# A fused attention and channel-mix kernel: its first wide product by Strassen's identity, with the tokens in rows of 512

## The chip, the cores and the metric

The kernel runs on one core of a Trainium2 chip. The metric is the device time of one launch in microseconds (us), taken as the median of several runs. The profiled execution is one launch more, whose trace gives the rows below.

The engines are called as in the profile: PE is TensorE (matmuls), PEld its weight loads, DVE is VectorE, ACT is ScalarE, POOL is GpSimd, and SP is the engine that issues the transfers (DMAs).

## The reference, cut to what matters

All data are float32, in 4 batches of 576 tokens, 512 channels wide.

```python
x = attention(q, k, v)                 # 8 heads, window 32, half of them dilated
xk = mu_k * x + (1 - mu_k) * x_prev    # xr alike, with mu_r
k = np.maximum(xk @ w_k, 0.0)          # 512 x 1024
x = sigmoid(xr @ w_r) * (k * k @ w_v)  # 512 x 512, 1024 x 512
h = x.transpose(0, 2, 1) @ U @ V       # 576 x 32, 32 x 576
u = x + h.transpose(0, 2, 1)
out = u + np.maximum(u @ w_ch1, 0.0) @ w_ch2   # 512 x 2048, 2048 x 512
```

The last line is phase two. Its two products are the widest of the kernel, and the first of them, `u @ w_ch1`, is the one that the change computes in another way.

## The kernel before

Channels lie on the partitions and tokens in the rows, so that a matmul takes 128 x 128 weights and as many columns as it has tokens. To keep float32 precision every operand is split into a high part (an ACT copy that rounds) and a low part (the difference, on DVE or POOL), and every product is three matmuls: high weights by high tokens, low by high, high by low (`mm3`, lines 309 to 311).

The tokens come in 8 half batches of 288 (`HS`, counted by `c`). Phase one does the attention and the products with w_r, w_k and w_v; its result y goes to DRAM (`ytmp`). U and V come between: for a batch, `load_y` reads y back (`yb`), `y_tr` transposes it (line 822), `u_mm` multiplies by U (lines 840, 841), and `v_mm` (line 855) multiplies by V and adds y, which gives u. Here u, its high part `uh` and its low part `ul` stay in SBUF.

Phase two is a loop over the 8 half batches and, within one, over the 16 blocks `f` of 128 hidden channels. `ch1(c, f)` is 12 matmuls 288 wide (4 pieces of 128 input channels, three matmuls each) into a PSUM bank of the kind `psM`. ACT takes the high part of its relu (line 894, `ch`), DVE the low part (line 895, `cl`). `ch2(c, f)` is 12 more matmuls, 3 for each of 4 output blocks (lines 914 to 916, four `psS` banks). It stands one block behind, so that ACT and DVE have the time of 24 matmuls. After the 16th block DVE adds u (line 922) and SP writes `ot` out (line 924). The split weights of both products are made once (`load_w2`, lines 298, 300, 303) and stay in SBUF for all half batches.

The order on each engine is not written by hand. Each operation goes on a list with a cost, and a planner (`plan`) deals the list out to five queues (PE, ACT, DVE, POOL, SP); each engine then works in that order and waits where an operand or a buffer isn't there yet. All transfers are issued by SP, one queue, in order. Buffers are taken in turn from pools: a tile with `bufs` of 2 waits for the readers of the one two before it.

Of the kernel before, what the change touches and what calls it, by code (L numbers as in the profile page):

```python
# [16 lines left out]
P = 128  # L17
# [41 lines left out]
W2RATE = 0.35  # L59
SPLIT = (-4, -4, -3, -3, -1, -1, 0, 0, 1, 1, 2, 2, 5, 5, 6, 6, 7, 7, 8, 8)  # L60
# [13 lines left out]
def tile_attention_mix_channel(  # L74
# [49 lines left out]
    def plan():  # L124
# [283 lines left out]
    def w2_part(i, part):
        t, c, _ = parts2[i][part]
        return t()[:, c : c + CW]  # L410

    def w2_keys(i, *parts):
        return [parts2[i][part][2] for part in parts]

    def load_w2(i, eng):
        st = Lazy([P, 2 * CW], F32, "w64", "wst", 4)
        dma(P * CW * 8, lambda: nc.sync.dma_start(st(), w2f[i]), [("w2f", i, 0), ("w2f", i, 1)], [(st,)])
        parts2[i] = [place2(4 * i + part) for part in range(4)]
        for j in range(2):
            hi_lo(CW, lambda j=j: st()[:, j * CW : (j + 1) * CW], [(st,)],  # L420
                  lambda j=j: w2_part(i, j), w2_keys(i, j), lambda j=j: w2_part(i, 2 + j), w2_keys(i, 2 + j), eng)
# [743 lines left out]
```

## Time and profile before

| | |
|---|---|
| median of the runs before | 793.4 us (790.64, 793.4, 795.26) |
| span of the profiled execution | 791.1 us |
| phase two begins | about 380 us |
| PE busy | 759.7 us, 96% of the span |
| DVE, ACT, POOL busy | 387.1, 326.0, 207.2 us |
| moved by DMA | 77.68 MB |

The span is the profiled execution's own time from its first to its last instruction. The runs are timed without a profile, and their median lies 2.3 us above this span. A busy PE means only that a matmul was under way: matmuls are pipelined, a new one starts long before the one ahead has ended, so the rate is read from the starts.

### The profile page before, as it was taken

How to read it: one execution, taken by the hardware profiler on the slowest of the kernel's cores; microseconds unless marked ns; L12 is line 12 of the kernel's file. 1: busy time of each engine (PE TensorE's matmuls, PEld its weight loads, DVE VectorE, ACT ScalarE, POOL GpSimd, SP SyncE). 2: the span in 40 equal slices, each digit the busy share in tenths (PEclk: the TensorE clock that was granted, in tenths of full speed). 3: DMA queues.
4: the chain of work that ended last, by engine and by line, in shares of the span. 5: the costliest groups of instructions: out<-in, count | busy, mean ns of one | idle time of the engine just before them, and what ended most of it. 6: DMA issues, size and time to landing. Idle time of an engine off the chain costs nothing.

```text
span 791.1 us, 16047 instructions
## 1 busy us (share of the span) xinstructions
PE 759.7 (96%) x6360; PEld 734.5 (93%) x6360; DVE 387.1 (49%) x1013; ACT 326.0 (41%) x875; POOL 207.2 (26%) x234
## 2 busy tenths in 40 slices
PE   5788999989999999999999999999999999999997
PEld 4566899989899999999999999999999999999997
DVE  5899999998989754464412322122221222221211
ACT  5577786767677676364311212112211112121110
POOL 1333365655465556292100011000101001010000
PEclk8999999999999999999999999999999999999999
DMA  8687348786777270128002000020000000000000
GB/s 256 201 244 221 106 134 236 236 254 193 243 218 224 92 248 1 44 94 276 28 1 90 1 31 2 1 90 1 1 31 1 30 2 1 31 2 1 31 1 31
DMA packets 34764, 77.68 MB, mean 98 GB/s; under 512 B 3968, under 2 KB 12288, under 8 KB 34688
## 3 DMA queue, kind: packets, MB, share of 16 engines
q1 hardware_dynamic: 34688, 76.65, 30.8%
q8 instruction: 50, 0.82, 0.4%
q14 instruction: 26, 0.21, 0.1%
HBM read 58.81 MB, written 17.83 MB: 97 GB/s over the span
## 4 chain that ended last, share of the span: by engine, by line
PE 80%; DVE 8%; ACT 6%; DMA 3%; issue 2%; POOL 1%; SPq 0%; DVEq 0%; ACTq 0%; POOLq 0%
PE psS L916 9%; PE psS L915 9%; PE psM L309 9%; PE psM L311 9%; PE psM L310 9%; PE psS L914 9%; PE psM L729 7%; PE psM L731 7%; PE psM L730 7%; ACT pr L594 2%; DMA w<-w1raw 2%; DVE wl L300 2%; PE psS L637 1%; PE psM L726 1%; PE psS L575 1%
## 5 line engine op out<-in xcount | busy, mean ns | idle before, releaser
L894 ACT ACTIVATE ch<-psM 128x288 fp32r<-128x288 f32 x128 | 52.6, 411 | 324.8 <-PE psM L311 322.8
L895 DVE SCALAR_TENSOR_TENSOR cl<-psM,ch 128x288 fp32r<-128x288 f32 x128 | 58.4, 456 | 248.5 <-ACT ch L894 248.5
L914 PE MATMUL psS<-ch,w 128*128 128x288 f32 x384 | 114.4, 298 | 0.0
L916 PE MATMUL psS<-cl,w 128*128 128x288 f32 x384 | 113.7, 296 | 0.0
L309 PE MATMUL psM<-uh,w 128*128 128x288 f32 x384 | 113.2, 295 | 0.0
L311 PE MATMUL psM<-ul,w 128*128 128x288 f32 x384 | 113.1, 295 | 0.0
L915 PE MATMUL psS<-ch,w 128*128 128x288 f32 x352 | 103.8, 295 | 0.0
L310 PE MATMUL psM<-uh,w 128*128 128x288 f32 x352 | 103.5, 294 | 0.0
L729 PE MATMUL psM<-xk,wh 128*128 128x288 f32 x336 | 101.2, 301 | 0.0
L731 PE MATMUL psM<-xk,wh 128*128 128x288 f32 x336 | 99.0, 295 | 0.9 <-POOL xk L298 0.9
L730 PE MATMUL psM<-xk,wl 128*128 128x288 f32 x336 | 99.2, 295 | 0.0
L914 PEld LDWEIGHTS psS<-ch,w 128*128 128x128 f32 x384 | 72.3, 188 | 0.0
L311 PEld LDWEIGHTS psM<-ul,w 128*128 128x128 f32 x384 | 72.2, 188 | 0.0
L916 PEld LDWEIGHTS psS<-cl,w 128*128 128x128 f32 x384 | 72.2, 188 | 0.0
L309 PEld LDWEIGHTS psM<-uh,w 128*128 128x128 f32 x384 | 72.2, 188 | 0.0
L729 PE MATMUL psM<-k2s,wh 128*128 128x288 f32 x224 | 67.1, 299 | 0.0
L298 POOL TENSOR_TENSOR ul<-u,uh 128x288 fp32r<-128x288 f32 x32 | 26.9, 842 | 151.8 <-ACT uh L303 151.8
L915 PEld LDWEIGHTS psS<-ch,w 128*128 128x128 f32 x352 | 66.3, 188 | 0.0
L310 PEld LDWEIGHTS psM<-uh,w 128*128 128x128 f32 x352 | 66.1, 188 | 0.0
L730 PE MATMUL psM<-k2s,wl 128*128 128x288 f32 x224 | 66.1, 295 | 0.0
L731 PE MATMUL psM<-k2s,wh 128*128 128x288 f32 x224 | 65.9, 294 | 0.0
L731 PEld LDWEIGHTS psM<-xk,wh 128*128 128x128 f32 x336 | 63.2, 188 | 1.4 <-POOL xk L298 1.4
(143 smaller groups left out, 1775.4 us busy)
## 6 DMA issues: line engine op xcount, KB each, us to landing
w<-w2raw SPq DMA_DIRECT2D x32, 512.0 KB, 5.6
w<-w1raw SPq DMA_DIRECT2D x20, 512.0 KB, 5.0
w2f<-w SPq DMA_DIRECT2D x32, 256.0 KB, 2.8
wst<-w2f SPq DMA_DIRECT2D x16, 512.0 KB, 4.2
raw<-qk SPq DMA_DIRECT2D x16, 320.0 KB, 6.3
ytmp<-y SPq DMA_DIRECT2D x32, 144.0 KB, 2.1
yb<-ytmp SPq DMA_DIRECT2D x4, 1152.0 KB, 5.8
out<-ot SPq DMA_DIRECT2D x32, 144.0 KB, 2.0
```

What stands on the lines that cost most here:

```text
L298: op("POOL", t, lambda: nc.gpsimd.tensor_tensor(out=out_(), in0=a(), in1=b(), op=ALU.subtract), r, w, 40, lock=True)
L309: nc.tensor.matmul(acc, lhsT=wh, rhs=xh, start=(i == 0), stop=False)
L310: nc.tensor.matmul(acc, lhsT=wl, rhs=xh, start=False, stop=False)
L311: nc.tensor.matmul(acc, lhsT=wh, rhs=xl, start=False, stop=(i == n - 1))
L729: nc.tensor.matmul(a, lhsT=wh, rhs=xh, start=start, stop=False)
L730: nc.tensor.matmul(a, lhsT=wl, rhs=xh, start=False, stop=False)
L731: nc.tensor.matmul(a, lhsT=wh, rhs=xl, start=False, stop=stop)
L894: act(HS, lambda: nc.scalar.activation(gh(), acc()[:, :HS], AF.Relu), [(acc,)], [(gh,)], psum=True)
L895: dve(HS, lambda: nc.vector.scalar_tensor_tensor(out=gl(), in0=acc()[:, :HS], scalar=0.0, in1=f32(gh()), op0=ALU.max, op1=ALU.subtract), [ ...
L914: nc.tensor.matmul(a, lhsT=wh, rhs=gh(), start=(f == 0), stop=False)
L915: nc.tensor.matmul(a, lhsT=wl, rhs=gh(), start=False, stop=False)
L916: nc.tensor.matmul(a, lhsT=wh, rhs=gl(), start=False, stop=(f == 15))
```

## The change

The tokens of all batches become one row of 2304, cut into a group of 256 and four of 512 (`GROUPS`). To be cut so, u goes to DRAM (`uf`, from a small tile `us` of two halves) and comes back by group (`ug`), and once more as `ot` where it is added to the output.

For a group of 512, `ch1(g, j)` computes two blocks of 128 hidden channels at once, j from 0 to 7. It takes the weights as 2 x 2 blocks (256 input channels by 128) and u as 2 x 2 blocks (256 channels by 256 tokens), and forms 7 products of sums and differences of the blocks where the plain way has 8. Each product is 6 matmuls 256 wide. DVE then combines the seven (with one ACT copy), and relu and the split follow, 512 wide. The group of 256 goes the plain way (`ch1_half`, with four products, 24 matmuls). `ch2` is 24 matmuls for a block, 512 wide (256 in the first group).

The sums of the weights do not fit in SBUF and are formed again for each block of each group (`load_cols`: two loads of 256 KB, DVE sums, ACT high parts, POOL low parts). The sums of u are formed once for a group (`operand`, seven of them). The weights of the second product stay in SBUF as before (`load_rows`).

U and V of two batches now stand in phase one (`side`, from the 10th step of the seventh half batch on) and those of the other two in the groups 1 and 2. The m, y, rt, k2 and d tiles of phase one become halves of one tile each, used in the same turns.

The diff, cut to its core:

```diff
+    w2st = {}
+    def stage2(f, j, tag="pr"):
+        t = w2st[f, j] = Lazy([P, CW], F32, tag, "st", 4 if tag == "pr" else 1)
+        dma(P * CW * 4, lambda: nc.sync.dma_start(t(), w2f[f][:, j * CW : (j + 1) * CW]), [("w2f", f, j)], [(t,)])
...
+    rows2_w = {}
+    def load_rows(f, eng):
+        stage2(f, 1, "pr" if f < 6 else ("y", "rt", "k2")[f % 3])
+        st = w2st.pop((f, 1))
+        h, l = rows2_w[f] = piece(F32R, "rh"), piece(F32R, "rl")
+        hi_lo(CW, lambda: st(), [(st,)], lambda: h(), [(h,)], lambda: l(), [(l,)], eng)
...
+    combos = {}
+    Q = 256
+    def load_cols(j, whole_set, eng):
+        stage2(2 * j, 0)
+        stage2(2 * j + 1, 0)
+        s1, s2 = w2st.pop((2 * j, 0)), w2st.pop((2 * j + 1, 0))
+        sm_ = Lazy([P, 5 * Q], F32, "sig", "sums", 1) if whole_set else Lazy([P, 2 * Q], F32, "w32", "sums", 3)
+        c52 = 1 if whole_set else 0
+        def q(t, n, k=1):
+            return lambda: t()[:, n * Q : (n + k) * Q]
+        def add(n, a, b, k, op_, key):
+            dve(k * Q, lambda: nc.vector.tensor_tensor(out=q(sm_, n, k)(), in0=a(), in1=b(), op=op_),
+                [(s1,), (s2,)], [(sm_, key)], two=True)
+        add(c52, q(s1, 0), q(s1, 1), 1, ALU.add, 5)
+        add(c52 + 1, q(s2, 0), q(s2, 1), 1, ALU.add, 2)
+        got = combos[j] = {}
+        got["h52"], got["l52"] = h, l = piece(F32R, "ch"), piece(F32R, "cl")
+        hi_lo(2 * Q, q(sm_, c52, 2), [(sm_, 5), (sm_, 2)], lambda h=h: h(), [(h,)], lambda l=l: l(), [(l,)], eng)
+        got["h34"], got["l34"] = h, l = piece(F32R, "ch"), piece(F32R, "cl")
+        for n, (st, m) in enumerate(((s1, 0), (s2, 1))):
+            hi_lo(Q, q(st, m), [(st,)], q(h, n), [(h, n)], q(l, n), [(l, n)], eng)
+        if not whole_set:
+            return
+        add(0, q(s1, 0), q(s2, 1), 1, ALU.add, 1)
+        got["1"] = h = piece(F32R, "ch")
+        hi_lo(Q, q(sm_, 0), [(sm_, 1)], q(h, 0), [(h, 0)], q(h, 1), [(h, 1)], eng)
+        add(3, q(s2, 0, 2), q(s1, 0, 2), 2, ALU.subtract, 6)
+        got["h67"], got["l67"] = h, l = piece(F32R, "ch"), piece(F32R, "cl")
+        hi_lo(2 * Q, q(sm_, 3, 2), [(sm_, 6)], lambda h=h: h(), [(h,)], lambda l=l: l(), [(l,)], eng)
...
+    uf = tc.dram_tile([P, 4, B * S], F32, name="uf")
+    ust = Lazy([P, 2 * HS], F32, "m", "us", 1)
...
+            out=u_(), in0=acc()[:, :HS], in1=y()[:, o, half * HS : (half + 1) * HS], op=ALU.add),
+            [(acc,), (y,)], [(ust, o % 2)], two=True, psum=True)
+        dma(P * HS * 4, lambda: nc.sync.dma_start(uf[:, o, c * HS : (c + 1) * HS], u_()), [(ust, o % 2)], [("uf", c, o)])
...
+    def load_ug(g):
+        t0, n = GROUPS[g]
+        x = ug[g] = Lazy([P, 4, n], F32, "x", "ug", 2)
+        dma(P * n * 16, lambda: nc.sync.dma_start(x(), uf[:, :, t0 : t0 + n]),
+            [("uf", c, o) for c in range(t0 // HS, (t0 + n - 1) // HS + 1) for o in range(4)], [(x,)])
...
+    def operand(g, n, eng):
+        x = ug[g]
+        h, l, (kh, kl) = operands[g, n] = slot()
...
+        if n in plain:
+            src, kx = blk(*plain[n]), [(x,)]
+        else:
+            tmp = Lazy([P, 2 * Q], F32, "w32", "tmp", 3)
+            a, b, how = {
+                1: ((0, 0), (1, 1), "add"), 3: ((0, 1), (1, 1), "sub"), 4: ((1, 0), (0, 0), "sub"),
+                6: ((0, 0), (0, 1), "add"), 7: ((1, 0), (1, 1), "neg"),
+            }[n] if g else {3: ((0, 0), (1, 0), "sub"), 4: ((1, 0), (0, 0), "sub")}[n]
+            src, kx = lambda: two(tmp()), [(tmp,)]
+            if how == "neg":
+                fn = lambda: nc.vector.scalar_tensor_tensor(
+                    out=src(), in0=blk(*a)(), scalar=-1.0, in1=blk(*b)(), op0=ALU.mult, op1=ALU.subtract)
+            else:
+                fn = lambda: nc.vector.tensor_tensor(
+                    out=src(), in0=blk(*a)(), in1=blk(*b)(), op=ALU.add if how == "add" else ALU.subtract)
+            dve(2 * Q, fn, [(x,)], kx, two=True)
+        copy(2 * Q, lambda: two(h()), src, kx, [kh])
+        sub(eng, 2 * Q, lambda: two(l()), src, lambda: two(f32(h())), kx + [kh], [kl])
...
+    ORDER = (5, 2, 3, 4, 1, 6, 7)
+    PLACE = {5: 0, 2: 1, 3: 0, 4: 1, 1: 0, 6: 0, 7: 1}
...
+    def product(g, j, ns, acc, at_):
+        parts = [(combo(j, n), operands[g, n], i) for n in ns for i in range(2)]
+        def run():
+            a = acc()[:, at_ * Q : (at_ + 1) * Q]
+            for k, ((wh, wl, _), (xh, xl, _), i) in enumerate(parts):
+                ci, wi = slice(i * Q, (i + 1) * Q), slice(i * P, (i + 1) * P)
+                nc.tensor.matmul(a, lhsT=wh()[:, wi], rhs=xh()[:, ci], start=(k == 0), stop=False)
+                nc.tensor.matmul(a, lhsT=wl()[:, wi], rhs=xh()[:, ci], start=False, stop=False)
+                nc.tensor.matmul(a, lhsT=wh()[:, wi], rhs=xl()[:, ci], start=False, stop=(k == len(parts) - 1))
+        pe(3 * len(parts) * MMQ, run, [k for c, o, i in parts if i == 0 for k in c[2] + o[2]], [(acc, at_)], "f32r")
...
+        product(0, j, (5, 3), acc, 0)
+        product(0, j, (2, 4), acc, 1)
...
+    def ch1(g, j):
+        if g == 0:
+            return ch1_half(j)
+        accs_ = {}
+        for n in ORDER:
+            if PLACE[n] == 0:
+                acc = bank("M")
+            accs_[n] = acc
+            product(g, j, (n,), acc, PLACE[n])
+        b52, a34, c1, d67 = accs_[5], accs_[3], accs_[1], accs_[6]
...
+        copy(2 * Q, lambda: sb(), lambda: b52(), [(b52, 0), (b52, 1)], [(sb,)], psum=True)
+        tt(2, lambda: cd(), lambda: a34(), lambda: sb(), ALU.add, [(a34, 0), (a34, 1), (sb,)], [(cd,)])
+        tt(1, half(gg, 0), half(a34, 1), half(sb, 0), ALU.subtract, [(a34, 1), (sb,)], [(gg, 0)])
+        tt(1, half(gg, 1), half(a34, 0), half(sb, 1), ALU.subtract, [(a34, 0), (sb,)], [(gg, 1)])
+        kg = [(gg, 0), (gg, 1)]
+        tt(2, lambda: two(gg()), lambda: two(gg()), lambda: c1()[:, :Q].unsqueeze(1).to_broadcast([P, 2, Q]), ALU.add,
+           [(c1, 0)] + kg, kg)
+        tt(1, half(gg, 0), half(gg, 0), half(d67, 1), ALU.add, [(d67, 1), (gg, 0)], [(gg, 0)])
+        tt(1, half(gg, 1), half(gg, 1), half(d67, 0), ALU.add, [(d67, 0), (gg, 1)], [(gg, 1)])
...
+    def ch2(g, j, hid):
...
+            acc = accs[g][o]
+            def run(o=o, acc=acc):
+                a = acc()[:, :n]
+                for e in range(2):
+                    wh, wl = (t()[:, o * P : (o + 1) * P] for t in rows2_w[2 * j + e])
+                    xh, xl = (t()[:, e * n : (e + 1) * n] for t in (hh, hl))
+                    nc.tensor.matmul(a, lhsT=wh, rhs=xh, start=(j == 0 and e == 0), stop=False)
+                    nc.tensor.matmul(a, lhsT=wl, rhs=xh, start=False, stop=False)
+                    nc.tensor.matmul(a, lhsT=wh, rhs=xl, start=False, stop=(j == 7 and e == 1))
...
+            pe(6 * (MMW if g else MMQ), run, [(t,) for e in range(2) for t in rows2_w[2 * j + e]] + kh, [(acc,)], "f32r")
+        if j < 7:
+            return
+        for o in range(4):
+            acc = accs[g][o]
+            ot = Lazy([P, n], F32, "d", "ot", 2)
+            dma(P * n * 4, lambda o=o, ot=ot: nc.sync.dma_start(ot(), uf[:, o, t0 : t0 + n]),
+                [("uf", c, o) for c in range(t0 // HS, (t0 + n - 1) // HS + 1)], [(ot,)])
+            dve(n, lambda acc=acc, ot=ot: nc.vector.tensor_tensor(out=ot(), in0=acc()[:, :n], in1=ot(), op=ALU.add),
+                [(acc,), (ot,)], [(ot,)], two=True, psum=True)
+            dma(P * n * 4, lambda o=o, ot=ot: nc.sync.dma_start(out[o, :, t0 : t0 + n], ot()), [(ot,)], [("out", g, o)])
...
+    side = [lambda: load_y(0)] + uv_u(0, "S", "S") + uv_v(0, "S") + uv_v(1, "S") + [lambda: load_y(1), lambda: load_ug(0)]
+    for fn, n in zip(uv_u(1, "S", "S"), (5, 3, 2, 4, 0, 0)):
+        side += [fn] + ([lambda n=n: operand(0, n, "POOL")] if n else [])
+    side += uv_v(2, "S") + uv_v(3, "S")
...
             if n in (VISIT0 if c == 0 else VISIT):
                 visit(2)
+            if c == NCH - 2 and n >= SIDE_AT:
+                side.pop(0)()
...
+    sides = {
+        1: [lambda: load_y(2)] + uv_u(2, "M", "M") + uv_v(4, "M") + uv_v(5, "M"),
+        2: [lambda: load_y(3)] + uv_u(3, "M", "M") + uv_v(6, "M") + uv_v(7, "M"),
+    }
...
+    for g in range(len(GROUPS)):
+        side = sides.get(g, [])
+        nxt = [lambda n=n: operand(g + 1, n, "POOL") for n in ORDER] if g + 1 < len(GROUPS) else []
+        if nxt:
+            nxt.insert(0, lambda: load_ug(g + 1))
+        todo, late = side + nxt[:6], nxt[6:]
+        for j in range(8):
+            hid = ch1(g, j)
+            if j == 7:
+                todo += late
+            for _ in range(3):
+                if todo:
+                    todo.pop(0)()
+            if g == 0:
+                if j + 3 < 8:
+                    load_cols(j + 3, False, "POOL")
+                    load_rows(2 * j + 6, "DVE")
+                    load_rows(2 * j + 7, "DVE")
+                elif j == 7:
+                    load_cols(0, True, "POOL")
+            elif (g, j) != (len(GROUPS) - 1, 7):
+                load_cols((j + 1) % 8, True, "POOL")
             if prev is not None:
                 ch2(*prev)
-            prev = (c, f, g)
+            prev = (g, j, hid)
+        for fn in todo:
+            fn()
     ch2(*prev)
```

On PE this is one block of the steady state before: a `ch1` of 12 (the last three of them are shown) and the first output blocks of a `ch2` (`psM` and `psS` are the banks, `uh` and `ul` the parts of u, `ch` and `cl` those of the hidden channels, `w2` the weights).

```order
L309 MATMUL psM_8961<-uh_8459,w2_4936 128x288
L310 MATMUL psM_8961<-uh_8459,w2_4955 128x288
L311 MATMUL psM_8961<-ul_8464,w2_4936 128x288
L914 MATMUL psS_8854<-ch_8948,w2_4912 128x288
L915 MATMUL psS_8854<-ch_8948,w2_4934 128x288
```

And this is the change at the same place: the end of a `ch2` of 24 for one block, and the start of the next block's 42 (`hh` and `hl` are the parts of the hidden channels, `rh` and `rl` the weights of the second product, `tr` the operands made of u, `ch` and `cl` now the sums of weights).

```order
L1070 MATMUL psS_7867<-hh_8422,rh_5388 128x512
L1071 MATMUL psS_7867<-hh_8422,rl_5408 128x512
L1072 MATMUL psS_7867<-hl_8438,rh_5388 128x512
L1070 MATMUL psS_7885<-hh_8422,rh_5378 128x512
L1071 MATMUL psS_7885<-hh_8422,rl_5386 128x512
L1072 MATMUL psS_7885<-hl_8438,rh_5378 128x512
L1070 MATMUL psS_7885<-hh_8422,rh_5388 128x512
L1071 MATMUL psS_7885<-hh_8422,rl_5408 128x512
L1072 MATMUL psS_7885<-hl_8438,rh_5388 128x512
L993 MATMUL psM_8590<-tr_4734,ch_8453 128x256
L994 MATMUL psM_8590<-tr_4734,cl_8462 128x256
```

The matmuls stay in the same turn of three; the rows of 288 columns have become rows of 256 in the first product and of 512 in the second.

On ACT this is the start of phase two before: copies of weights (line 303, `wst` is the loaded tile) and the first relu (line 894) among them.

```order
L303 ACTIVATE w2A_4999<-wst_5003 128x512 x2
L894 ACTIVATE ch_5074<-psM_5040 128x288
L303 ACTIVATE w2_5099<-wst_5035 128x512
L303 ACTIVATE w2_5104<-wst_5035 128x512
L894 ACTIVATE ch_5110<-psM_5082 128x288
```

The same place now (line 307 are the copies, line 1007 the relu of the group of 256; `ug_5055` is u of group 1, `tmp` its sums, `st` and `sums` are weights).

```order
L1007 ACTIVATE hh_5039<-psM_4985 128x512
L307 ACTIVATE rh_5044<-st_4763 128x512
L307 ACTIVATE tA_5127<-ug_5055 128x512 x2
L307 ACTIVATE tA_5127<-tmp_5125 128x512
L307 ACTIVATE tA_5127<-tmp_5146 128x512
L1007 ACTIVATE hh_5163<-psM_5024 128x512
L307 ACTIVATE tB_5172<-tmp_5165 128x512
L1007 ACTIVATE hh_5174<-psM_5112 128x512
L307 ACTIVATE ch_5221<-sums_5197 128x512
```

Copies of the next group's operands now stand ahead of two relus of the group of 256.

On SP this is the end of the program before: the last four writes of a result, with the two ahead of them.

```order
L924 DMA out<-ot_8847 128x288
L924 DMA out<-ot_8850 128x288
L924 DMA out<-ot_9286 128x288
L924 DMA out<-ot_9291 128x288
L924 DMA out<-ot_9297 128x288
L924 DMA out<-ot_9300 128x288
```

And now: between the writes stand loads of u (line 1080), and the tiles of the third and fourth of them have the buffers of the first two.

```order
L1080 DMA ot_9051<-uf_91 128x512
L1080 DMA ot_9053<-uf_91 128x512
L400 DMA st_9066<-w2f14_84 128x512
L400 DMA st_9068<-w2f15_85 128x512
L1084 DMA out<-ot_9051 128x512
L1084 DMA out<-ot_9053 128x512
L1080 DMA ot_9488<-uf_91 128x512
L1080 DMA ot_9490<-uf_91 128x512
L1084 DMA out<-ot_9488 128x512
L1084 DMA out<-ot_9490 128x512
```

The last write thus stands behind two loads that stand behind two writes.

## Rows read from the trace of the kernel before

**Rows 1.** The page: busy time, and the span in 40 slices of 20 us

```profile
PE 759.7 (96%) x6360; PEld 734.5 (93%) x6360; DVE 387.1 (49%) x1013; ACT 326.0 (41%) x875; POOL 207.2 (26%) x234
...
PE   5788999989999999999999999999999999999997
...
PEclk8999999999999999999999999999999999999999
```

**Rows 2.** Busy time by stretch: length, engines, granted clock, DMA share, GB/s

```profile
core 0: us, PE busy (x) PEld busy (x) DVE busy (x) ACT busy (x) POOL busy (x), PEclk, DMA share, GB/s
...
240.00:280.00 40.00, 40.00 (x422) 39.28 (x421) 31.50 (x104) 28.07 (x86) 21.63 (x24) 1.00 0.53 170
...
360.00:380.00 20.00, 20.00 (x153) 20.00 (x152) 11.77 (x22) 11.09 (x22) 3.65 (x4) 1.00 0.72 259
...
480.00:520.00 40.00, 40.00 (x304) 40.00 (x304) 7.41 (x17) 6.75 (x17) 3.23 (x4) 1.00 0.00 1
```

**Rows 3.** Timeline of phase two: start, duration (us), engine, line

```profile
562.66 0.29 PE L309 MATMUL psM<-uh,w 128*128 128x288 f32 x1
562.66 0.19 PEld L310 LDWEIGHTS psM<-uh,w 128*128 128x128 f32 x1
...
564.24 0.30 PE L855 MATMUL psM<-vs,g 128*128 128x288 f32 x1
```

**Rows 4.** Timeline of a step of U in phase one

```profile
330.54 0.40 PE L840 MATMUL psS<-yh,us 128*128 128x512 f32 x1
...
330.77 0.39 PE L841 MATMUL psS<-yl,us 128*128 128x512 f32 x1
...
331.00 0.60 PE L822 MATMUL psS<-cst_t,yb 128*128 128x128 f32 x4
```

**Rows 5.** Groups by line and shape, 380 to 790 us: count, busy, mean ns

```profile
L895 DVE SCALAR_TENSOR_TENSOR cl<-psM,ch 128x288 fp32r<-128x288 f32 x122 | 55.6, 456 | 245.0 <-ACT ch L894 245.0
...
L298 POOL TENSOR_TENSOR ul<-u,uh 128x288 fp32r<-128x288 f32 x27 | 21.7, 805 | 141.3 <-ACT uh L303 141.3
...
L922 DVE TENSOR_TENSOR ot<-psS,u 128x288 f32<-128x288 f32 x32 | 12.4, 448 | 1.1 <-PE psS L916 1.1
...
L300 DVE TENSOR_TENSOR yl<-psM,yh 128x512 fp32r<-128x512 f32 x12 | 8.3, 691 | 6.6 <-ACT yh L303 6.6
...
L822 PE MATMUL psM<-cst_t,yb 128*128 128x128 f32 x48 | 7.2, 272 | 0.0
L303 ACT ACTIVATE yh<-psM 128x512 fp32r<-128x512 f32 x12 | 7.2, 598 | 4.6 <-DVE cl L895 3.0 <-PE psM L822 1.6
```

**Rows 6.** The same groups, 0 to 380 us

```profile
L298 POOL TENSOR_TENSOR xk<-m,xk 128x288 fp32r<-128x288 f32 x56 | 54.8, 988 | 21.6 <-ACT xk L303 16.0 <-issue 2.9 <-POOL k2s L298 1.3
...
L298 POOL TENSOR_TENSOR w<-wst,w 128x512 fp32r<-128x512 f32 x12 | 16.1, 1356 | 18.5 <-PE psM L731 10.2 <-ACT w L303 8.3
```

**Rows 7.** DMA issues of the page: count, KB each, us to landing

```profile
w2f<-w SPq DMA_DIRECT2D x32, 256.0 KB, 2.8
...
ytmp<-y SPq DMA_DIRECT2D x32, 144.0 KB, 2.1
yb<-ytmp SPq DMA_DIRECT2D x4, 1152.0 KB, 5.8
out<-ot SPq DMA_DIRECT2D x32, 144.0 KB, 2.0
```

**Rows 8.** Timeline of the end of the span

```profile
785.74 1.63 DVE L922 TENSOR_TENSOR ot<-psS,u 128x288 f32<-128x288 f32 x4 [1.09 <-PE psS L916]
...
786.58 0.29 PE L916 MATMUL psS<-cl,w2B 128*128 128x288 f32 x1
```

More of the change, by code (lines that the diff above doesn't have):

```diff
@@ L160, in x_end @@
         def x_end(x):
+            if x.end is not None:
+                return x.end
             end = 0.0
@@ L165, in x_end @@
                 end = max(end, u.done)
+            x.end = end
             return end
@@ L181, in ready @@
                     return None
-                ends = sorted((x_end(y) for y in x.line[max(0, x.at - 4 * x.bufs) : x.at]), reverse=True)
+                ends = sorted((x_end(y) for y in x.line[: x.at]), reverse=True)
                 if len(ends) >= x.bufs:
@@ L408, in w2_part @@
[L408 to L421, printed above, removed]
+    w2st = {}
@@ new lines, in combo @@
+    def combo(j, n):
+        c = combos[j]
+        if n == 1:
+            t = c["1"]
+            return (lambda: t()[:, :Q]), (lambda: t()[:, Q:]), [(t, 0), (t, 1)]
+        which, half = {5: ("52", 0), 2: ("52", 1), 3: ("34", 0), 4: ("34", 1), 6: ("67", 0), 7: ("67", 1)}[n]
+        h, l = c["h" + which], c["l" + which]
+        keys = [(h, half), (l, half)] if which == "34" else [(h,), (l,)]
+        return (lambda: h()[:, half * Q : (half + 1) * Q]), (lambda: l()[:, half * Q : (half + 1) * Q]), keys
@@ L663, in attend2, with half_slot @@
         yield
-    dd = {}
+    dd = set()
+    turn = dict.fromkeys(("m", "y", "rt", "k2"), 0)
+    halves = {t: Lazy([P, 2 * HS], F32, t, t, 1) for t in turn}
+    dt_ = [Lazy([P, 2 * HS], F32, "d", "d", 2) for _ in range(2)]
+    def half_slot(tag):
+        t, i = halves[tag], turn[tag] % 2
+        turn[tag] += 1
+        return lambda: t()[:, i * HS : (i + 1) * HS], (t, i)
     def mix(c, p, which):
@@ new lines, in tile_attention_mix_channel, with slot @@
+    GROUPS = ((0, Q),) + tuple((Q + 2 * Q * g, 2 * Q) for g in range(4))
+    ug = {}
+    def load_ug(g):
[3 more added lines that the diff above has]
+            [("uf", c, o) for c in range(t0 // HS, (t0 + n - 1) // HS + 1) for o in range(4)], [(x,)])
+    homes = {}
+    operands = {}
+    nslot = 8
+    def slot():
+        nonlocal nslot
+        n = nslot % 12
+        nslot += 1
+        if n < 8:
+            tag = "AB"[n // 4]
+            if tag not in homes:
+                homes[tag] = Lazy([P, 16 * Q], F32R, tag, "t" + tag, 1)
+            t, c = homes[tag], n % 4 * 4 * Q
+        else:
+            if n not in homes:
+                homes[n] = Lazy([P, 4 * Q], F32R, "raw", "tr", 4)
+            t, c = homes[n], 0
+        return (lambda: t()[:, c : c + 2 * Q]), (lambda: t()[:, c + 2 * Q : c + 4 * Q]), [(t, n, "h"), (t, n, "l")]
@@ L1033, in tile_attention_mix_channel @@
     convert_to(len(jobs))
-    load_y(0)
-    load_w2(0, "POOL")
-    side = uv_u(0, "S", "S") + uv_v(0, "S")
+    prep = {}
+    for j in range(3):
+        at_ = (0, 5, 12)[j]
+        prep[at_] = lambda j=j: load_cols(j, False, "POOL")
+        prep[at_ + 1] = lambda j=j: load_rows(2 * j, "DVE")
+        prep[at_ + 2] = lambda j=j: load_rows(2 * j + 1, "DVE")
     for i, fn in enumerate(quanta(NCH - 1)):
         fn()
-        if i >= 1 and side:
+        if side:
             side.pop(0)()
-        if i in (4, 5, 6):
-            load_w2(i - 3, "POOL")
-        if i in (12, 13, 14, 15, 16):
-            load_w2(i - 8, "POOL" if i - 12 in (1, 3, 5) else "DVE")
+        if i in prep:
+            prep[i]()
```

148 lines of the change are left out of this document (55 added, 93 removed).

## The prediction

> **What bounds it now.** I read the page's busy times and slices first. PE is busy 96% of the span, and from about 180 us on the nines run without a gap to the last slice, with the granted clock at nine tenths or more [rows 1]. The table by stretch comes next: in 480 to 520 PE is busy for all of its 40 us, while DVE, ACT and POOL work for 7.41, 6.75 and 3.23 us and the transfers rest [rows 2]. So phase two is worth what its matmuls are worth, and nothing else in it is near a limit. But "busy" doesn't give the price of one matmul. That is the pitch from start to start: the 12 matmuls of a `ch1` begin between 562.66 and 564.24, which is 1.58 us or 132 ns each [rows 3], and 304 in 40 us give the same [rows 2]. The weight load runs for 190 ns under the matmul ahead of it and starts every 132 ns too, so it takes no time of its own at this width.
>
> **PE's columns.** Phase two had 8 x 16 x 24 = 3072 matmuls of 288 columns: 3072 x 0.132 = 405.5 us. Now the group of 256 has 8 x 48 = 384 matmuls 256 wide, the four others have 4 x 8 x 42 = 1344 of 256 and 4 x 8 x 24 = 768 of 512. Counted by columns that is 884,736 before and 835,584 now, 5.6% less, and fewer matmuls by 19%.
>
> No row shows a 256-wide matmul. The 512-wide ones of U are 0.23 us apart (330.54, 330.77, 331.00) [rows 4]. The line through 288 at 132 and 512 at 230 rises 0.4375 ns a column, and gives 132 - 32 x 0.4375 = 118 ns at 256. The bounds are 132, if narrower rows gain nothing, and 109, which is the pitch of four transposes 128 wide, each with a weight load of its own: they take 0.60 us together and one 0.27 [rows 4, 5], so three pitches are 0.33. Weight loads can thus follow each other every 109 ns, and don't hold a pitch of 118. I take the line. Now: 1728 x 0.118 + 768 x 0.230 = 203.9 + 176.6 = 380.5 us. **PE: -25.0 us** (-40 to -1 by the bounds).
>
> At this place the Trainium skill has a formula (TensorE: Matmul & The Clock Gate, "Back-to-back issue gap"): columns divided by 2.4, plus 2.5 ns. It would make 122.5, 109.2 and 215.8 ns, hence 376.3 us before, 354.4 now, and -21.9. The trace's 132 and 230 ns are longer, and the measurement decides.
>
> The matmuls of U and V are the same ones elsewhere. PE is without a gap in 240 to 280 and in 360 to 380 alike [rows 2], so two batches' U and V moved into phase one give nothing and cost nothing.
>
> **The other engines, block by block.** A block of a 512 group is 42 x 0.118 + 24 x 0.230 = 10.5 us of PE. Beside it stand:
> - POOL, the low parts of the sums of weights: two subtractions of 512 columns at 1.356 [rows 6] and three of 256. Between 0.805 at 288 [rows 5] and 1.356 the line gives 0.73, so 4.9 us. Each must wait for ACT's high part (0.6 for 512) and the first for DVE's sum; with that a turn is 6.2. The seven operands of the next group, 1.36 each, come in the last three blocks, 3.2 us a block: 9.4 of 10.5.
> - DVE: from 0.448 at 288 and 0.691 at 512 [rows 5], 0.41 at 256. Sums of weights 3 x 0.41 + 0.69, combining 2 x 0.69 + 4 x 0.41, two low parts of 0.69: 6.3 us.
> - ACT: seven copies or relus of 512 or 256 columns at 0.6 [rows 5] or less: 4.2.
>
> All are covered while PE's block lasts 10.5. The chain from product 7 to the `ch2` that needs it is two additions of 256, a relu and a low part, 2 x 0.41 + 0.6 + 0.69 = 2.1 us and some handovers, under the 5.5 us of the `ch2` that stands between. So steady blocks add **0**; were the cover gone, a stall would be what a turn takes over 10.5.
>
> **The start of phase two.** Group 1 needs u of batch 1: the last V tiles are added (0.45), written to DRAM (2.1 [rows 7]), two tiles at a time because `us` has two halves, so twice, and then 1 MB is read (5.8 for 1152 KB [rows 7]): 2 x (0.45 + 2.1) + 5.8 = 10.9 us. Four ACT copies (0.6 each) stand ahead of a relu of the group of 256 in ACT's queue, and behind it waits PE: 13.3, with handovers 15. PE has 8 x 0.132 + 144 x 0.118 = 18 us of work from those V to the `ch2` concerned, so 3 us are clear. What waits in the queue behind is all of ACT's work for that group, weights too. The transfers are the second risk: 32 weight loads of 256 KB and 2.2 MB of y and u are 10.6 MB in about 57 us (12 of phase one and the 45 of group 0), or 186 GB/s. The trace shows 259 GB/s in 360 to 380 and 170 in 240 to 280 [rows 2]; at 170 it takes 62 us, 5 too many. I take **+2** (0 to 10: both at once).
>
> **The end.** Before, PE's last matmul ends at 786.58 + 0.29 = 786.87 and the last addition at 785.74 + 1.63 = 787.37 [rows 8]; the span ends at 791.1, 4.2 us after PE and 3.7 after DVE. Now let E be PE's end. `ot` has two buffers, so the fourth load of u waits for the landing of the second write, and SP does nothing else meanwhile. The second output block is complete two blocks before the end, E - 12 x 0.23 = E - 2.8; its addition (0.69) ends at E - 2.1, its write (2.8 for 256 KB [rows 7]) lands at E + 0.7, the load at E + 3.5, the addition ends at E + 4.2. Then comes what follows the last addition today, 3.7, and 0.8 more since the write is 256 KB and not 144 (2.8 against 2.0 [rows 7]): E + 8.7. That is **+4.5** against 4.2. Without any wait for buffers it would be +2 (larger addition and write); with each of the transfers a third slower, +7. I take 4.
>
> **Sum** against the profiled 791.1: -25 + 0 + 2 + 4 = -19, so 772. The runs' median lies 2.3 above this span: **774 us**.
>
> **The rivals.**
> - *The start of phase two stalls* (the reading of u later than 18 us after its V, or weights late): by its bound 8 us more than I took, and a few us of later group changes, 782 to 789. For it: one SP queue in order, and no transfer of before sat in such a chain. Against it: 3 us clear, and 259 GB/s seen. 17%.
> - *The pitch stays at 132 for 256 columns* (something other than the columns sets it, as the 109 ns at 128 columns shows that something does): 1728 x 14 ns = 24 us less gain, 796 to 798. It decides at 118 + 19 / 1.728 = 129 ns. For it: nothing measured at 256. Against it: the floor of 109 and the fall from 230 to 132. Strassen would then do nothing for the time, its seven products costing what eight would by the line. 7%.
> - *Slower: POOL becomes the bound at each change of group.* A POOL subtraction of 288 columns takes 988 ns beside a busy DVE and 805 beside an idle one [rows 5, 6]. If they exclude each other fully, DVE's work on two SBUF operands (sums 1.9, low parts 1.4) adds to POOL's 4.9: 8.2 a block, and in the last three blocks of a group, with 3.2 of POOL and 1.2 of DVE for operands, 12.6, so 2.1 over PE's 10.5 in each: up to 6 us late at each of four changes: +24, 798. It ends slower than before from a turn of about 12.2 us in those 12 blocks (19 / 12 = 1.6 over 10.5). Against it: the row shows 1.23 times, not a block, and 9.4 x 1.23 = 11.6 in three blocks is 3 us a change at worst, if no block before had run ahead. 7%.
> - *Nothing stalls and the end hides*: 762 to 768. 5%.
>
> The Trainium skill names that exclusion (SBUF — State Buffer, "SBUF: two separate sides"): DVE and GpSimd share a port pair as an exclusive lock, which a DVE operation with two SBUF inputs takes against GpSimd for its whole length. The trace's 988 against 805 is no full block, but those rows don't show how far the two were offset in time.
>
> **How the numbers follow.** The forecast, 768 to 781 with the bounds of the start and the end, has 64%. The range reaches into the first rival and to the better case, 766 to 790, for 8 in 10. Half a per cent of 793.4, 4 us, is about what a measurement of this kernel can tell from no change. Faster by more (under 789.4): the forecast, the first rival and the better case, 86%. Slower by more (over 797.4): half of the second and third and what I haven't seen, 8%. Between: 6%.
>
> **What would show it.** Right: the 256-wide starts 118 ns apart, the 512-wide 230; blocks of 10.5 us with PE at 40 of 40 in phase two; some us of idle PE ahead of group 0's later `ch2` or none; 8 to 9 us from PE's last matmul to the end of the span, with two loads of u and their waits in them. Wrong: a 256 pitch over 125; PE's idle time put down to POOL at the changes of group; ACT waiting on the read of u while PE waits for a relu; or phase one longer than 380 us, since I moved U and V there for nothing.

## The result, and the profile after the change

The changed kernel takes 780.0 us (median of 4 runs, 778.1 to 782.03) against 792.88 before (4 runs, 790.64 to 795.26): a ratio of 0.9841, with a 95% interval of 0.9812 to 0.9871. The span of the profiled execution is 776.3 us, where it was 791.1.

The page's busy times and slices, to be laid beside [rows 1]:

```profile
PE 740.8 (95%) x5784; PEld 680.5 (88%) x5784; DVE 560.4 (72%) x1301; ACT 410.1 (53%) x1019; POOL 391.5 (50%) x404
...
PE   5779799999999999999999999999999999999996
```

PE does fewer matmuls and stays the bound; DVE has 173 us more work and POOL 184 more. The pitch is read from starts again, here for the first product with operands in a large tile (`tB`), then in a small one (`tr`), and for the second product:

```profile
639.72 0.28 PE L994 MATMUL psM<-tB,cl 128*128 128x256 f32 x1
...
641.40 0.28 PE L993 MATMUL psM<-tr,ch 128*128 128x256 f32 x1
...
642.11 0.40 PE L1070 MATMUL psS<-hh,rh 128*128 128x512 f32 x1
...
642.81 0.39 PE L1070 MATMUL psS<-hh,rh 128*128 128x512 f32 x1
```

14 matmuls in 1.68 us are 120 ns, the six behind them 118, and three of 512 columns in 0.70 us 233. By stretch (busy us of each engine, as in [rows 2]) PE is full where the weights are formed again, also across a change of group (560 to 600):

```profile
560.00:600.00 40.00, 40.00 (x257) 36.19 (x256) 33.48 (x51) 18.85 (x38) 31.62 (x28) 1.00 0.27 91
640.00:680.00 40.00, 40.00 (x249) 36.00 (x248) 23.33 (x48) 16.33 (x32) 22.07 (x21) 1.00 0.21 67
```

What PE waited for from 370 to 460 us (in total, times, longest); from 450 us on the same view names no wait of PE at all:

```profile
PE psM L994 <- POOL cl L302: 1.3, 3, 0.6
PE psS L1072 <- DVE hl L1008: 0.7, 1, 0.7
PE psS L1070 <- DVE us L906: 0.6, 1, 0.6
PE psM L901 <- DVE g L304: 0.3, 1, 0.3
```

The timelines of ACT and POOL at that place. ACT's first copy of group 1's u and the POOL operation behind it have waited 5.80 and 14.94 us for the read of u; POOL then has five operands at some 1.5 us each before it comes to `cl`, the low parts of weights that PE waits for:

```profile
384.37 1.15 ACT L307 ACTIVATE tA<-ug 128x512 fp32r<-128x512 f32 x2 [5.80 <-DMA ug<-uf]
...
385.08 3.01 POOL L302 TENSOR_TENSOR tA<-ug,tA 128x512 fp32r<-128x512 f32 x2 [14.94 <-ACT tA L307]
388.04 2.98 POOL L302 TENSOR_TENSOR tA<-tmp,tA 128x512 fp32r<-128x512 f32 x2
390.99 1.47 POOL L302 TENSOR_TENSOR tB<-tmp,tB 128x512 fp32r<-128x512 f32 x1
393.49 1.29 POOL L302 TENSOR_TENSOR cl<-sums,ch 128x512 fp32r<-128x512 f32 x1 [1.02 <-ACT ch L307]
```

DVE at the same place: an addition of V that waited for a write of u, and the low part of a hidden block (`hl`) behind the sums of group 1's u (`tmp`):

```profile
377.43 0.46 DVE L906 TENSOR_TENSOR us<-psS,yb 128x288 f32<-128x288 f32 x1 [2.75 <-DMA uf<-us]
...
385.34 3.29 DVE L975 TENSOR_TENSOR tmp<-ug 128x512 f32<-128x512 f32 x2
388.56 0.68 DVE L1008 SCALAR_TENSOR_TENSOR hl<-psM,hh 128x512 fp32r<-128x512 f32 x1
```

And the end, to be laid beside [rows 8]: PE's last matmul, and DVE's last two additions with the waits for the loads of u.

```profile
769.35 0.39 PE L1072 MATMUL psS<-hl,rh 128*128 128x512 f32 x1
...
771.14 0.69 DVE L1082 TENSOR_TENSOR ot<-psS,ot 128x512 f32<-128x512 f32 x1 [3.47 <-DMA ot<-uf]
772.60 0.69 DVE L1082 TENSOR_TENSOR ot<-psS,ot 128x512 f32<-128x512 f32 x1 [0.77 <-DMA ot<-uf]
```

The span ends at 776.3: 6.6 us after PE, 3.0 after DVE.

**Where the time went.** To keep the attention steps out of it I measure from a mark in phase one, the start of the 400th product matmul after the first (line 729 before, 772 after), which is at 289.1 us before and 291.0 after. From there to the end the trace has, in us:

| | before | after | difference | predicted |
|---|---|---|---|---|
| starts of `ch1` and `ch2` added up, without waits | 406.7 | 382.6 | -24.1 | -25 |
| waits among them (starts over 8 ns late) | 1.3 | 4.9 | +3.7 | +2 |
| transposes, U and V | 21.0 | 22.1 | +1.2 | 0 |
| end, after PE's last matmul | 4.2 | 6.6 | +2.4 | +4 |
| mark to end of the span | 502.0 | 485.4 | -16.6 | -19 |
| the mark itself | 289.1 | 291.0 | +1.9 | 0 |

The rest between mark and end, some 69 us of phase one's last products and attention, is the same in both.

### The profile page after: what moved, and what is told of

Same layout as the page of the kernel before. It is cut to its first block, busy times and chain, and to the rows that moved or that the text cites. A ratio compares the mean times of both kernels' runs of the same rounds, so it can differ in the third digit from the quotient of the medians.

```text
span 776.3 us, 16122 instructions
## 1 busy us (share of the span) xinstructions
PE 740.8 (95%) x5784; PEld 680.5 (88%) x5784; DVE 560.4 (72%) x1301; ACT 410.1 (53%) x1019; POOL 391.5 (50%) x404
## 4 chain that ended last, share of the span: by engine, by line
PE 63%; DVE 14%; DMA 9%; ACT 6%; issue 4%; POOL 3%; SPq 0%; DVEq 0%; POOLq 0%; ACTq 0%
PE psS L1072 7%; PE psS L1070 7%; PE psS L1071 7%; PE psM L994 7%; PE psM L993 7%; PE psM L995 7%; PE psM L772 5%; PE psM L774 5%; PE psM L773 5%; DMA w<-w1raw 2%; POOL cl L302 2%; ACT pr L629 2%; DMA w2f<-w 2%; DVE w L344 1%; DVE w L347 1%
## 5 line engine op out<-in xcount | busy, mean ns | idle before, releaser
L302 POOL TENSOR_TENSOR cl<-sums,ch 128x512 fp32r<-128x512 f32 x72 | 102.3, 1421 | 103.8 <-ACT ch L307 71.1
L1070 PE MATMUL psS<-hh,rh 128*128 128x512 f32 (+1 forms) x320 | 119.5, 374 | 0.6 <-DVE us L906 0.6
L1072 PE MATMUL psS<-hl,rh 128*128 128x512 f32 (+1 forms) x320 | 119.1, 372 | 0.7 <-DVE hl L1008 0.7
L1071 PE MATMUL psS<-hh,rl 128*128 128x512 f32 (+1 forms) x320 | 118.7, 371 | 0.0
L427 DVE TENSOR_TENSOR sums<-st 128x256 f32<-128x256 f32 (+1 forms) x144 | 75.4, 566 | 13.4 <-POOL cl L302 12.2
L1030 DVE TENSOR_TENSOR ort<-psM,oy 128x512 f32<-128x512 f32 x32 | 22.1, 690 | 83.1 <-PE psM L995 59.6
L302 POOL TENSOR_TENSOR cl<-st,ch 128x256 fp32r<-128x256 f32 x80 | 62.1, 797 | 30.1 <-PE psM L995 21.3
L1072 PEld LDWEIGHTS psS<-hl,rh 128*128 128x128 f32 x320 | 60.2, 188 | 11.7 <-DVE hl L1008 0.9
L1071 PEld LDWEIGHTS psS<-hh,rl 128*128 128x128 f32 x320 | 60.3, 188 | 9.7
L772 PEld LDWEIGHTS psM<-xk,wh 128*128 128x128 f32 x336 | 63.0, 188 | 0.8
L774 PEld LDWEIGHTS psM<-xk,wh 128*128 128x128 f32 x336 | 63.2, 188 | 0.3 <-POOL xk L302 0.3
L773 PEld LDWEIGHTS psM<-xk,wl 128*128 128x128 f32 x336 | 63.1, 188 | 0.1
```

The costliest lines, as they stand in the source:

```text
L302: op("POOL", t, lambda: nc.gpsimd.tensor_tensor(out=out_(), in0=a(), in1=b(), op=ALU.subtract), r, w, 40, lock=True)
L427: dve(k * Q, lambda: nc.vector.tensor_tensor(out=q(sm_, n, k)(), in0=a(), in1=b(), op=op_), [(s1,), (s2,)], [(sm_, key)], two=True)
L772: nc.tensor.matmul(a, lhsT=wh, rhs=xh, start=start, stop=False)
L773: nc.tensor.matmul(a, lhsT=wl, rhs=xh, start=False, stop=False)
L774: nc.tensor.matmul(a, lhsT=wh, rhs=xl, start=False, stop=stop)
L1070: nc.tensor.matmul(a, lhsT=wh, rhs=xh, start=(j == 0 and e == 0), stop=False)
```

## The experiments

Each was an edit of the changed kernel, but for the last, which is the kernel before. "From the mark" is the time from that same matmul to the end of the span in the run's profile, 485.4 for the change; it agreed within 0.2 us between the two profiles of the kernel before, whose runs spread over 6 us, and within 0.5 between the change and e7_align, an edit that moves no work.

**Four output tiles in the last group** (e1_four_ot).

```diff
             ot = Lazy([P, n], F32, "d", "ot", 2)
+            if g == len(GROUPS) - 1 and o >= 2:
+                ot = Lazy([P, n], F32, "m", "ot", 1) if o == 2 else Lazy([P, n], F32, "x", "ot", 2)
```

> The edit: in the last group the third and fourth output tile get buffers of their own, so their loads of u needn't wait for the first two writes. Theory (the end is a wait for buffers): in the profile of the change DVE stands idle 3.47 us for the load of the third tile after PE's last matmul, and the span ends 6.6 us after PE. Without that wait the last addition ends about 0.8 us after PE and the write takes 3.0, so the span ends 3.9 us after PE: 2.7 us less, 777.3 for the median of 780.0. Rival (the larger last write sets the end and the loads hide in it): less than 0.5 us less.

776.19 us, ratio to before 0.9783 (0.9762 to 0.9805). From the mark 483.4, 2.0 less. DVE's timeline, the last addition:

```profile
772.18 0.69 DVE L1084 TENSOR_TENSOR ot<-psS,ot 128x512 f32<-128x512 f32 x1 [0.70 <-PE psS L1072]
```

DVE waits only for PE now (whose last matmul ends at 772.14), and the span ends 3.8 us after PE and not 6.6: 2.8 us, as expected. The end was a wait for buffers. From the mark it is less, mostly because PE waited 3.6 us at the start of phase two in this profile and 2.9 in the change's.

**The operands of group 1 later** (e2_later).

```diff
-                if todo:
+                if todo and (g or j >= 3):
                     todo.pop(0)()
```

> The edit: the reading of group 1's u and its seven operands go on the list at the fourth to sixth block of group 0 and not at its first. Theory (the start of phase two waits for the read of u: POOL idle 14.9 us for the first operand and the low parts of weights queued behind it late, three waits of PE for them, and one for the low part of a hidden block behind the same operands in ACT's and DVE's queues): these four waits of PE, some 2.7 us with their restarts, go; the one of 0.76 us at 377 us stays, since it is a wait for a write of u. 2 to 3 us less, 777 to 778. Rival (the weights are late because their own loads are, with 32 of them in SP's one queue): the waits stay with a load as releaser, no change. A second rival: the operands come too late for group 1 then, and PE waits at the change of group instead.

776.67 us, 0.9792 (0.9768 to 0.9815). From the mark 482.0, 3.3 less. All that PE waits for from 370 to 460 us is now this, where the change had four lines:

```profile
PE psS L901 <- DVE us L906: 0.4, 1, 0.4
```

The low parts of weights come ahead of the operands in POOL's order, and the operands are still in time for group 1. So the waits came from the order of the queues, not from a shortage of POOL or of transfers.

**U and V five steps earlier** (e3_early).

```diff
-SIDE_AT = 9
+SIDE_AT = 4
```

> The edit: U and V of the first two batches start five steps earlier in the seventh half batch. Theory (the chain of V, write of u and read of u is what is late at the start of phase two): group 1's u is read some 8 to 10 us earlier, before group 0's blocks need ACT and POOL, so that all of the 3.5 us of PE's waits between 377 and 420 us go: 776.5 to 778. Rival (POOL and DVE are simply short of time there, in whatever order): the waits move, less than 1 us changes. Second rival: phase one has no room for U and V that early, its own attention steps wait, and the time rises by 1 to 4 us.

776.45 us, 0.9786 (0.9771 to 0.9801), but from the mark 484.2, only 1.2 less; the rest of the lower median is an earlier mark (289.4). PE's waits from 340 to 460 us:

```profile
PE psS L884 <- DVE yl L304: 0.5, 2, 0.3
PE psS L1070 <- DVE us L906: 0.4, 1, 0.4
PE psS L1072 <- DVE hl L1008: 0.3, 1, 0.3
```

The wait for POOL is gone, which bears the chain of V, write and read out; but U itself now makes PE wait in phase one, which is the second rival in part. The expectation held for the cause and not for the amount.

**The sums of weights not formed again** (e4_keep_sums).

```diff
-            elif (g, j) != (len(GROUPS) - 1, 7):
-                load_cols((j + 1) % 8, True, "POOL")
+            elif g == 1 and j < 7:
+                load_cols(j + 1, True, "POOL")
...
-    def combo(j, n):
+    def combo(g, j, n):
-        c = combos[j]
+        c = combos[j if g < 2 else 7]
```

> Left out here: in the groups 2 to 4 no sums of weights are loaded, formed or split; every block uses those of the last block of group 1. Theory (the rebuilding is covered by PE's block and costs nothing, as PE is without a gap from 450 us on): the time stays within 1 us of the change, and the pitch of the 256-wide matmuls stays at 120 ns for operands in the two large tiles and 118 for the small ones, since it goes with where an operand lies. Rival (the rebuilding on DVE, ACT, POOL and the DMAs slows PE's reads of SBUF): the pitch falls to 118 or below everywhere and 2 to 4 us are gained. Second rival (POOL and DVE hold PE up at the changes of group): more than 4 us are gained.

779.96 us, 0.9832 (0.9816 to 0.9848); from the mark 487.2, 1.9 more than the change and not less. All but 0.2 of that arose ahead of what was left out or behind PE's last matmul: from the first product of group 2 to the start of the last matmul it takes 264.51 us here and 264.29 in the change, and the groups 3 and 4 take 84.27 and 90.13 us in both. In two stretches of it:

```profile
600.00:640.00 40.00, 40.00 (x248) 36.00 (x247) 19.72 (x38) 6.85 (x11) 0.00 (x0) 1.00 0.17 53
...
720.00:760.00 40.00, 40.00 (x254) 36.10 (x253) 14.05 (x28) 7.04 (x12) 0.00 (x0) 1.00 0.00 1
```

POOL rests, PE issues as many matmuls as before (247 to 256 in 40 us, from 560 to 760 us, against 249 to 257), and the pitch stays at 120 in the large tiles. Forming the sums again is fully covered.

**Groups of 512 without Strassen** (e5_plain). `ch1` becomes two plain blocks; `load_plain` splits the two blocks of weights, and the operands are four rows of u:

```diff
+        for e in range(2):
+            acc = bank("M")
+            wh, wl = combos[j][e]
+            xs = [operands[g, k] for k in range(4)]
+            def run(acc=acc, wh=wh, wl=wl):
+                mm3(acc(), [(wh()[:, k * P : (k + 1) * P], wl()[:, k * P : (k + 1) * P], xs[k][0](), xs[k][1]()) for k in range(4)])
...
-                load_cols((j + 1) % 8, True, "POOL")
+                load_plain((j + 1) % 8, "POOL")
```

> The edit: groups of 512 the plain way, without Strassen: per block 24 matmuls of 512 columns in place of 42 of 256, no sums of u and none of weights (the splits of the weights stay, 2 of 512 a block). All else as in the change. Theory (the gain is PE's columns, and Strassen's seventh product fewer is nearly all of it): 32 blocks x (24 x 0.232 - 42 x 0.1195) = 17.6 us more on PE; the waits at the start of phase two stay about the same: 796 to 798, so that rows of 512 alone would be worth about nothing against before (793). Rival (what the sums cost on the other engines eats a part of Strassen's gain): less than 12 us more, under 792.

788.44 us, 0.9933 (0.9908 to 0.9959). From the mark 495.2: 9.8 more than the change, where 17.6 was expected. The time is on the rival's side (under 12 more, under 792). But the columns cost less than I reckoned, too, since the 512-wide matmuls were faster here: 176 in 40 us or 227 ns in this stretch, and 229 in the mean, where the change has 231 in the mean without its waits.

```profile
640.00:680.00 40.00, 40.00 (x176) 32.82 (x175) 4.84 (x7) 8.07 (x15) 9.15 (x7) 1.00 0.13 43
```

The starts of `ch1` and `ch2` add up to 397.3 us, of which 0.7 are waits; in the change they add up to 387.5, of which 4.9 are waits. Without the waits the plain way thus takes 14.0 more, and its waits are 4.2 less: 9.8, as measured. PE waited once that the view names, for 0.9 us. So most of the change's waits at the start of phase two are part of Strassen's price, as the rival had it. Transposes, U and V take 22.1 us in both; their 1.2 over the kernel before don't come from Strassen. All of the change but Strassen is worth 502.0 - 495.2 = 6.8 us, not nothing, and Strassen 9.8 as built, some 13 without the waits (against the 482.0 of e2_later).

**More work for POOL** (e6_pool_more).

```diff
+        for _ in range(2):
+            sub(eng, 2 * Q, lambda l=l: l(), q(sm_, 3, 2), lambda h=h: f32(h()), [(sm_, 6), (h,)], [(l,)])
```

> The edit: two more subtractions of 512 columns on POOL for each block's weights in the groups 1 to 4 (each forms the same low part again). Theory (POOL's turn has cover: 2 x 1.42 + 3 x 0.79 = 5.2 us measured, with the two 8.0, with handovers about 9.3, under PE's 10.5; in the last three blocks of a group with 3.5 us of operands 12.8, 2.3 too many): no wait of PE in the first five blocks of a group, some waits at the ends of groups 1 to 3, 0 to 20 us in all, since weights are formed one block ahead: 780 to 800. Rival (DVE and POOL exclude each other, so the turn is already near its end): waits in every block, over 25 us more.

811.35 us (one run); from the mark 519.6, 34 more. PE's longest waits from 440 us on, and three stretches:

```profile
PE psS L1073 <- ACT hh L1052: 9.0, 6, 2.2
PE psM L997 <- POOL cl L303: 5.7, 7, 1.9
```

```profile
500.00:506.00 6.00, 4.47 (x12) 3.29 (x13) 4.47 (x7) 2.70 (x6) 2.87 (x4) 0.72 0.00 1
...
600.00:640.00 40.00, 32.64 (x168) 26.50 (x168) 23.93 (x39) 14.31 (x29) 33.82 (x28) 0.87 0.23 76
640.00:680.00 40.00, 39.41 (x250) 35.51 (x250) 28.68 (x50) 15.31 (x32) 30.55 (x28) 1.00 0.13 45
```

The place was as in the first theory, the size not: it lies beyond that theory's 20 and on the rival's side (over 25). Ordinary blocks hardly wait (640 to 680), the changes of group do (group 3 begins at 622). From 340 us on the waits add up to 23.7 us, where the change has 2.9. The granted clock falls after them, to 0.72 and 0.87 in the first two stretches; by these shares that costs at most another 0.28 x 6 + 0.13 x 40 = 6.9 us. POOL isn't full over those 40 us (33.82): it waits 1.1 to 2.8 us in each block for a high part from ACT. Between these waits it works without a pause, so that the trace shows in-order queues out of slack, and not which single engine would have to be faster.

**Tiles at multiples of 64 bytes** (e7_align).

```diff
-    mu_t = cp.tile([P, 8], F32, name="mu_t")
+    mu_t = cp.tile([P, 16], F32, name="mu_t")[:, :8]
```

> The edit: a small constant tile is 64 bytes a partition and not 32, so that every tile behind it starts at a multiple of 64 bytes; before and after the change they all start at 32 past one. Theory (the pitch of a matmul goes with where its operand lies: in the change 120 ns with operands in the two large tiles, which start at 32 past a multiple of 1024, and 118 or 113 in the small ones): the pitch changes for all tiles, by some ns; if it falls to 113 everywhere, 1728 x 6 = 10 us less, if to 110, 15 us less. Rival (columns set the pitch, and the differences between tiles have another cause): 118 to 120 stay, no change, 779 to 781.

777.51 us, 0.9795 (0.977 to 0.9821), and from the mark 485.9, 0.5 more: no gain. The pitch in `tB` is 120 ns as before (641.83 to 642.91 are 9 matmuls in 1.08 us). The theory fell; such a shift isn't what makes the large tiles slower.

```profile
641.83 0.28 PE L994 MATMUL psM<-tB,cl 128*128 128x256 f32 x1
...
642.91 0.28 PE L994 MATMUL psM<-tB,cl 128*128 128x256 f32 x1
```

**Both waits taken away** (e8_both): the edits of e1_four_ot and e2_later together.

> Both edits that took a wait away: four output tiles in the last group, and group 1's operands three blocks later. Theory (the two waits are at different places and add up): from the 400th product of phase one to the end of the span 485.4 us in the change become 479 (2.8 less at the end, 3.4 less at the start of phase two), 774 for the median. Rival (they don't add, since an earlier end of the blocks finds the transfers late): 776 to 777 as with either.

773.17 us (770.6 to 775.46, 5 runs), 0.9729 (0.9702 to 0.9757). From the mark 479.7, 5.7 less than the change, with 3.8 at the end: the two add up. One wait of PE is left from 340 us on, for the write of u:

```profile
PE psS L901 <- DVE us L906: 1.2, 1, 1.2
```

**Four tiles for u as well** (e9_four_us), on top of these two.

```diff
+    ust2 = Lazy([P, 2 * HS], F32, "d", "us", 2)
...
-        u_ = lambda: ust()[:, o % 2 * HS : (o % 2 + 1) * HS]
+        ut = ust2 if c in (2, 3) and o >= 2 else ust
+        u_ = lambda: ut()[:, o % 2 * HS : (o % 2 + 1) * HS]
```

> The kernel with both edits, and a third: the tiles of u on their way to DRAM are four and not two while batch 1 goes through V. Theory (the one wait of PE that is left, 1.2 us for a V tile whose DVE addition waits for the write of u two tiles before, is a wait for that buffer): it goes, from the 400th product of phase one to the end 478.4 us and not 479.7, 772 for the median. Rival (the writes themselves are late in SP's queue): the wait stays or moves to the read of group 1's u; no change.

773.41 us, 0.9747 (0.972 to 0.9773); from the mark 479.0, 0.7 less than with two edits, where 1.3 was expected. The wait for `us` is gone from the view and another of 0.3 us stands in it. That is too little for the times to tell; that the wait went is told by the view alone.

**The kernel before once more** (e10_before).

> The kernel before, unchanged, for a second profile of it. Theory (phase one is the same in both kernels, and the 1.9 us by which its 400th product came later after the change is the scatter of the first 120 us from execution to execution): the 400th product of phase one (at 289.1 us in the first profile, 289.4 to 294.3 in those of the changed kernels) comes anywhere in 289 to 295, and from there to the end it takes 502.0 again, within 0.5. Rival (halves of tiles slow phase one): 289 again.

793.62 us; the mark at 290.0 and 501.8 us from there to the end. The marks in the ten profiles of changed kernels lay between 289.4 and 294.3, 291.6 in the mean, so the scatter is larger than the 1.9 us. But both marks of before are early ones, so that a phase one slower by 1 or 2 us can't be excluded; this stays open.

## Why the prediction was right

The forecast was 774 in a range of 766 to 790, and faster at 86%; 780.0 came from the forecast mechanism, with two terms mis-sized, one each way. (The bounds of the start and the end, 0 to 10 and 2 to 7, give 770 to 785; the 768 to 781 that the 64% were put on don't follow from them.)

- **The columns** carried it. The line through two pitches gave 118 and 230 ns where the trace has 118 to 120 and 232 to 233 (231 in the mean), and -25.0 against -24.1 measured. The rival of a pitch that stays at 132 fell in the first profile. By the Trainium skill's formula (TensorE: Matmul & The Clock Gate, "Back-to-back issue gap"), which the page gives for an isolated matmul, 109 and 216 ns and an estimate of -21.9 would have come out; the trace has some 10 ns more on the one and 16 on the other.
- **Steady blocks add nothing**: shown twice, by the empty view of waits from 450 us on and by e4_keep_sums, whose groups 3 and 4 take the change's time to the hundredth of a us.
- **The start of phase two** was mis-sized: +2 stood in the sum, +3.7 in `ch1` and `ch2` and +1.2 with U, V and transposes were measured. I had followed the chain (V, write, read, copies in ACT's queue) and found 3 us clear for the relu of the group of 256. Two things were missing in it. Behind the operands in POOL's queue stood the low parts of weights, which PE needed sooner than that relu; I named POOL's work, but priced it only in its steady blocks. And DVE's queue was left out: an addition of V that waited 2.75 us for a write of u keeps the PSUM bank that `ch2` is to use (0.6 us of PE), and the low part of a hidden block stands behind the sums of group 1's u (0.7). e2_later showed that the order was the cause, and took 3.3 of it back.
- **The end** was mis-sized the other way: +4 in the sum, +2.4 measured. The wait for two buffers was there as told, the additions within 0.7 us of their forecast places (the last one ends at E + 3.6, not E + 4.2). But from the last addition to the end of the span it took 3.0 us, and not 3.7 + 0.8, though the write is larger. Why it took 3.7 before, with four writes issued close together, was not tested. The +2 for an end without any wait was too much as well: its rows give 0.2 for the addition and 0.8 for the write, and e1_four_ot, which took 2.8 back, ended 3.8 us after PE, 0.4 less than before.
- **The rest of the 6 us** between 774 and 780 is no step of the sum: the mark 1.9 us later, and a median 3.7 us above the span of the profiled run where I took 2.3. The timed runs lie some 1.8 above their own spans, and the profiled execution is one of them, with 778.1 the fastest of four; so the other 1.9 of the 3.7 is scatter between runs.
- **POOL as the bound** stayed a rival. Its count of three late blocks in a group doesn't hold for group 3: no U and V stand there, so five operands of group 4 come at its front (592 to 608 us), right behind the last of group 3's own. And DVE and POOL do get in each other's way: in 460 to 760 us of the changed kernel a low part on DVE with both operands in SBUF takes 1018 ns (that of the block's other half 796), and the same operation 692 in 600 to 640 us of e4_keep_sums, where POOL rests. Within the change's trace, the 11 of the 27 beside which no POOL operation ran took 687 in the mean, the other 16 took 1245. An addition of that width with one operand in PSUM takes 690 in the change and 692 in e4_keep_sums. The first two rows are the change's, the other two those of e4_keep_sums:

```profile
L1050 DVE SCALAR_TENSOR_TENSOR hl<-ok,hh 128x512 fp32r<-128x512 f32 x27 | 27.5, 1018 | 1.6 <-ACT hh L1049 1.4
...
L1030 DVE TENSOR_TENSOR ort<-psM,oy 128x512 f32<-128x512 f32 x28 | 19.3, 690 | 76.1 <-PE psM L995 57.1 <-ACT ch L307 14.6 <-ACT oy L307 3.5
```

```profile
L1050 DVE SCALAR_TENSOR_TENSOR hl<-ok,hh 128x512 fp32r<-128x512 f32 x4 | 2.8, 692 | 1.5 <-ACT hh L1049 1.4
L1030 DVE TENSOR_TENSOR ort<-psM,oy 128x512 f32<-128x512 f32 x4 | 2.8, 692 | 14.8 <-PE psM L995 11.2 <-ACT oy L307 3.6
```

The Trainium skill's exclusive lock (SBUF — State Buffer, "SBUF: two separate sides") would hold just such operations up; a mean of 1.5 times, with those beside no POOL operation at 687, agrees with some of them waiting, and e6_pool_more shows how little more the changes of group could bear.

## What to carry to other kernels

When an engine bounds a kernel for hundreds of microseconds, price the change by the pitch from start to start at two sizes; the line through them held to 2 ns here, at a third size just outside the two. The error sits in the seams: follow every in-order queue past the late transfer and ask what the next engine needs from behind it, not only what waits for the transfer itself. Work that is covered can still be issued in the wrong order; moving it three blocks later gave back as much as any buffer.

## What the runs showed of the hardware

- The pitch of a 256-wide matmul goes a little with the tile of its operand: 120 ns in the two large tiles, 118 in the small ones, and 113 or 114 for some runs of some 23 matmuls there. The 120 and 118 don't depend on what DVE and POOL do (e4_keep_sums), and the 120 not on tiles that start at multiples of 64 bytes (e7_align). The 113 isn't fixed by the tile: in group 0 it comes in some profiles and not in others. The cause is open.
- 512-wide matmuls were 229 ns apart in the mean without Strassen (e5_plain) and 231 with it, both at a granted clock of 1.00; that, too, is open.
- A DVE operation of 512 columns on two operands in SBUF took 1245 ns in the mean when a POOL operation ran beside it and 687 when none did (the change, 460 to 760 us); one with an operand in PSUM took 690 there and 692 where POOL rested (e4_keep_sums).
- After PE had waited 2.2 us in e6_pool_more, the granted clock was 0.72 in 500 to 506 us, and two 512-wide starts there are 0.42 us apart, which is the pitch of the lower of its two levels (1.2 GHz):

```profile
502.85 0.63 PE L1073 MATMUL psS<-hh,rh 128*128 128x512 f32 x1
503.27 0.63 PE L1074 MATMUL psS<-hh,rl 128*128 128x512 f32 x1
```
